# Attention for eight batches with a two-layer feed-forward: four heads in 32-row tiles, turned by 32x32 block transposes, laid out by a list scheduler

## The chip, the cores and the metric

One core of a Trainium2 chip runs the kernel. Its engines each work through an instruction queue of their own, in order: TensorE (PE in the profile; its weight loads are shown apart as PEld), VectorE (DVE), ScalarE (ACT), GpSimd (POOL), and SyncE (SP), which issues most DMAs. The metric is the device time of one execution in microseconds (us).

## What is computed

The reference, cut to what matters:

```python
# q, k, v: (8 batches, 12 heads, 448 tokens, 64); w_in: (768, 2048); w_out: (2048, 768)
q_n = q / np.sqrt(np.mean(q * q, -1, keepdims=True) + 1e-06) * g_q      # k_n likewise with g_k
scores = np.matmul(q_n, k_n.transpose(0, 1, 3, 2)) / 8
attn = softmax(scores)
x = np.matmul(attn, v).transpose(0, 2, 1, 3).reshape(3584, 768)
h = x @ w_in
out = (np.maximum(h, 0) + alpha * np.minimum(h, 0)) @ w_out
```

## The kernel before

**Groups.** The twelve heads of a batch are worked on in three groups of four (`G = 3`), so there are 24 groups, numbered y = 0 to 23; the tokens form seven blocks of 64 (`J = 7`). For a group, `load_qk` brings q and k to SBUF with one DMA each on SP's queue, `square` squares them (mostly POOL), `reduce` sums over the 64 elements of a head (VectorE), `root` makes 1/rms (ScalarE), and `scale` multiplies (POOL, for the first groups VectorE). The scaled `qs` must then be turned, with the head's 64 elements on partitions, into `qkT`. Group 0 has its own versions with the prefix `part_`.

**Turning.** For y below 7 (`TD`) TensorE transposes 14 blocks per group against the identity into a PSUM bank (lines 256, 285, 330), and VectorE copies the banks out, q with a copy (272, 291, 337) and k with a multiply by the combined gain (266, 295, 339). From y = 7 on `turn_dma` (line 304) issues two DMA transposes from SP, and `turn` multiplies k by the gain in place (line 315).

**Attention.** `score` (line 357) makes, for one group and one block of 64 keys, four heads' scores against all 448 queries: four matmuls of 64 rows by 64 columns of the array up to y = 8, and eight of 64 by 32 from y = 9 (`EARLY`). They run side by side. `soft` (371) is the exponential on ScalarE. `over_keys` (382) multiplies the exponentials by ones, which gives the denominators (`den`, tile `dn`), or by v (`attv`, tiles `av` and `avb`), in tiles of 64 rows by 32 columns. Two groups of a batch are summed as a pair, the third alone; for the third one `ones_over` (406) works on half the columns. `log` and `invert` (434, 439, 429) make 1/denominator on ScalarE, and VectorE multiplies it in and writes `xT` (464, 481).

**Feed-forward.** `up(b, ft)` (line 496) is six full-array matmuls for 128 of the 2048 hidden columns of batch b, in bank `hT` (or `hTa`, `hTb`); ScalarE multiplies by alpha (536) and VectorE takes the larger of the two (540) into `gT`, which holds two batches. `down` (558) is a direct product of 16 matmuls for a tile of 128 tokens and half of the output columns. From tile 6 on, pairs of tiles share seven half products of eight matmuls instead of eight (`quad_a`, `quad_b`, `quad_c`, and `quad` for the last tiles; line 623); POOL and VectorE make the sums that these need (`mix_two`, `mix_rest`, `mix_weights`). Results go out through tiles `osb` and SP.

**Order.** The work is written out burst by burst: each burst n holds two, seldom three or four, score tiles and perhaps a denominator or a value sum, and `gaps[n]` holds the feed-forward units behind it, given by a count of time for batches 0 and 1 and by a table after that. `prep`, `post`, `jobs`, `late` and `after` place the work of the other engines. Five direct products stand between batch 0's and batch 1's hT. Before the data is there TensorE runs `spin` matmuls on zeros.

PSUM has two tiles of two banks for scores (`sc`), one of two banks for sums (`acc`), and two of one bank (`mm`).

Of the kernel before, what the change touches and what calls it, by code (L numbers as in the profile page):

```python
# [21 lines left out]
def kernel(  # L22
# [18 lines left out]
    HH = H // 2  # L41
    G = HH // 2
# [6 lines left out]
    TD = min(7, NG)  # L49
    EB = 3  # L50
    EARLY = 3 * G
    PRE = 3 * G - 1
    assert G == 3

# [11 lines left out]
    q4, k4, v4 = (  # L66
        t.rearrange("b (h g) (p j) d -> b (g p) h (j d)", g=2, j=J) for t in (q, k, v)
    )
    out4 = out.rearrange("(b p j) m -> b j p m", b=B, j=J)

# [10 lines left out]
    cols = cst.tile([128, NF + 2], FP32, name="cols", tag="cols")  # L81
    alpha_sb = cols[:, :NF]
    gain = cst.tile([128, 1], FP32, name="gain", tag="gain")
# [11 lines left out]
    MIXED = 2 * G + 1  # L95
    arena = cst.tile([128, (3 * HB + 3 * SB) // 4], FP32, name="arena", tag="arena")

    def lent(start, size):

        return arena[:, start // 4 : (start + size) // 4]  # L100
# [5 lines left out]
    nat, sqs, qs, ss_t, rr_t, qkT, vt, xT = {}, {}, {}, {}, {}, {}, {}, {}  # L106
    SRC = {"q": q4, "k": k4}


    rows = lent(0, 512)[: NF + 2]  # L110

    def load_qk(y, hold=False):
        b, i = divmod(y, G)
        for nm in "qk":
            if y in (2, 5, 8):
                t = lent(HB + "qk".index(nm) * NB4, NB4).rearrange(
                    "p (h j d) -> p h j d", h=2, j=J
                )
            else:
                t = ld.tile([128, 2, J, D], FP32, name="nat", tag="nat", bufs=4)  # L120
            if hold and nm == "q":

                nc.scalar.copy(out=t[:, 0, 0, 0:1], in_=expb)
            o = t.rearrange("p h j d -> p h (j d)")
            for h in range(2) if (y, nm) == (0, "q") else (slice(0, 2),):
                nc.sync.dma_start(out=o[:, h], in_=SRC[nm][b, :, ds(2 * i, 2)][:, h])
            nat[y, nm] = t

    def load_v(b):
        t = att.tile([128, HH, J, D], FP16, name="vt", tag="vt", bufs=1)  # L130
        nc.gpsimd.dma_start(out=t.rearrange("p h j d -> p h (j d)"), in_=v4[b])
        vt[b] = t

    def block_of(g, i):
        return 2 * g + i if i < 2 else 4 + g

    def load_w_in(c):

        src = moe_w_in[:512].rearrange("(n x p) f -> n p x f", n=4, p=32)
        for n in range(4):  # L140
            nc.gpsimd.dma_start(
                out=w_in_sb[ds(32 * n, 32), :4, ts(c, FB)], in_=src[n, :, :, ts(c, FB)]
            )
        if c % 2 == 0:
            w = ts(c // 2, 2 * FB)
            src = moe_w_in[512:].rearrange("(n g e p) f -> e n p g f", n=2, g=2, e=2)
            for e in range(2):
                for n in range(2):
                    nc.gpsimd.dma_start(
                        out=w_in_sb[ds(64 * e + 32 * n, 32), 4:, w], in_=src[e, n, :, :, w]  # L150
                    )
# [11 lines left out]
    def square(y, nm):  # L163
        src = nat[y, nm].rearrange("p h j d -> p (h j d)")
        if y % 2 and y < 3 * G + 1:
            sq = lent(HB + (2 + "qk".index(nm)) * NB4, NB4).rearrange("p (n d) -> p n d", d=D)
        else:
            sq = ld.tile([128, 2 * J, D], FP32, name="sq", tag="sq", bufs=2)
        sqf = sq.rearrange("p n d -> p (n d)")
        if (y, nm) == (1, "q"):  # L170
            nc.scalar.activation(out=sqf, in_=src, func=AF.Square)
        else:

            n = 2 if (y, nm) in ((2, "q"), (G, "k")) else 1
            for h in range(n):
                c = ts(h, 2 * J * D // n)
                nc.gpsimd.tensor_mul(out=sqf[:, c], in0=src[:, c], in1=src[:, c])  # L177
        sqs[y, nm] = sq

    def reduce(y, nm, heads=None):  # L180
        if y not in ss_t:
            ss_t[y] = ld.tile([128, 2, 2, J], FP32, name="ss", tag="ss", bufs=4)
        o = ss_t[y][:, "qk".index(nm)].rearrange("p h j -> p (h j)").unsqueeze(2)
        for c in [slice(0, 2 * J)] if heads is None else [ts(h, J) for h in heads]:
            nc.vector.tensor_reduce(  # L185
                out=o[:, c], in_=sqs[y, nm][:, c], axis=AXIS_X, op=ALU.add
            )

    def root(y, nms="qk"):
        n = len(nms)  # L190
        at = "qk".index(nms[0])
        if at == 0:
            rr_t[y] = ld.tile([128, 2, 2, J], FP32, name="rr", tag="rr", bufs=4)
        rr, ss = rr_t[y][:, ds(at, n)], ss_t[y][:, ds(at, n)]
        nc.scalar.activation(out=rr, in_=ss, func=AF.Ln, scale=1.0 / D, bias=RMS_EPS)
        nc.scalar.activation(out=rr, in_=rr, func=AF.Exp, scale=-0.5)

    def scale(y, nm):
        if y in (1, 3, 5):
            t = lent(HB + 4 * NB4 + "qk".index(nm) * NB4 // 2, NB4 // 2).bitcast(FP16)  # L200
            t = t.rearrange("p (j h d) -> p j h d", j=J, h=2)
        else:
            t = ld.tile([128, J, 2, D], FP16, name="qs", tag="qs", bufs=2)
        eng = nc.vector if y < G or (y, nm) == (G, "q") else nc.gpsimd
        eng.tensor_mul(  # L205
            out=t.rearrange("p j h d -> p h j d"),
            in0=nat[y, nm],
            in1=rr_t[y][:, "qk".index(nm)].unsqueeze(3).broadcast_to((128, 2, J, D)),
        )
        qs[y, nm] = t  # L210


    tops = {}

    def part_square(nm, h, j, eng):
        if ("sq", nm) not in tops:
            tops["sq", nm] = ld.tile([128, 2 * J, D], FP32, name="sq", tag="sq", bufs=2)
        o = tops["sq", nm].rearrange("p (h j) d -> p h j d", h=2)[:, h, j]
        src = nat[0, nm][:, h, j]
        if eng is nc.scalar:  # L220
            nc.scalar.activation(out=o, in_=src, func=AF.Square)
        else:
            eng.tensor_mul(out=o, in0=src, in1=src)

    def part_reduce(nm, h, j):
        if 0 not in ss_t:
            ss_t[0] = ld.tile([128, 2, 2, J], FP32, name="ss", tag="ss", bufs=4)
        nc.vector.tensor_reduce(
            out=ss_t[0][:, "qk".index(nm), h, j].unsqueeze(3),
            in_=tops["sq", nm].rearrange("p (h j) d -> p h j d", h=2)[:, h, j],  # L230
            axis=AXIS_X, op=ALU.add,
        )

    def part_root(nm, j):
        if 0 not in rr_t:
            rr_t[0] = ld.tile([128, 2, 2, J], FP32, name="rr", tag="rr", bufs=4)
        n = "qk".index(nm)
        rr, ss = rr_t[0][:, n, :, j], ss_t[0][:, n, :, j]
        nc.scalar.activation(out=rr, in_=ss, func=AF.Ln, scale=1.0 / D, bias=RMS_EPS)
# [154 lines left out]
    def cols_of(ys):  # L394
        return S // 2 if halved(ys) else S
# [834 lines left out]
```

## Time and profile before

| | |
|---|---|
| median of 2 runs (range) | 413.1 us (412.56 to 413.63) |
| profiled execution: time, span | 414.78 us, 413.0 us |
| mean granted TensorE clock | 0.995 |
| instructions: TensorE, VectorE, ScalarE, GpSimd | 5055, 420, 390, 184 |
| one exponential (line 371), 168 of them | 913 ns |
| slope and max of one hT (lines 536, 540) | 633 and 623 ns |
| one square, one scale on POOL (177, 205) | 1681 and 1713 ns |
| one reduce on VectorE, 896 elements (185) | 1077 ns |
| copy of a turned q, gain multiply of a turned k from PSUM (337, 339) | 621 and 676 ns |
| gain multiply of k turned by DMA (315), 17 of them | 1135 ns |
| DMA transposes, 17 of q and 17 of k, to landing | 2.9 and 3.7 us |
| loads of q or k, 448 KB, to landing | 4.9 to 8.5 us |

The span runs from the first to the last instruction of the profiled execution. A row of instructions gives the mean duration of one. Since matmuls overlap, their durations add to more than the time that they take; the distance from one start to the next says more. A name in brackets behind a row is what ended the engine's idle time before it.

### The profile page before, as it was taken

How to read it: one execution, taken by the hardware profiler on the slowest of the kernel's cores; microseconds unless marked ns; L12 is line 12 of the kernel's file. 1: busy time of each engine (PE TensorE's matmuls, PEld its weight loads, DVE VectorE, ACT ScalarE, POOL GpSimd, SP SyncE). 2: the span in 40 equal slices, each digit the busy share in tenths (PEclk: the TensorE clock that was granted, in tenths of full speed). 3: DMA queues.
4: the chain of work that ended last, by engine and by line, in shares of the span. 5: the costliest groups of instructions: out<-in, count | busy, mean ns of one | idle time of the engine just before them, and what ended most of it. 6: DMA issues, size and time to landing. Idle time of an engine off the chain costs nothing.

```text
span 413.0 us, 11724 instructions
## 1 busy us (share of the span) xinstructions
PE 398.9 (97%) x5055; PEld 208.1 (50%) x5055; DVE 266.9 (65%) x420; ACT 257.3 (62%) x390; POOL 255.8 (62%) x184
## 2 busy tenths in 40 slices
PE   7889999899999999999999999999999999999996
PEld 3344445444456445554455445545555455645664
DVE  3876875476567388785688585958576755465322
ACT  5697787567846785557766786875657783135110
POOL 5599996589677969376373847484724407300870
PEclk9899999999999999999999999999999999999999
DMA  8999899957754894329861697279332700320143
GB/s 259 231 217 206 172 200 155 248 169 103 163 81 134 204 169 91 115 63 197 144 168 48 173 138 177 63 180 193 59 75 54 127 3 24 75 59 0 30 103 97
DMA packets 67330, 53.38 MB, mean 129 GB/s; under 512 B 34880, under 2 KB 66768, under 8 KB 67280
## 3 DMA queue, kind: packets, MB, share of 16 engines
q1 hardware_dynamic: 53344, 40.45, 40.5%
q0 software_dynamic: 13536, 11.81, 21.5%
q8 instruction: 39, 0.64, 0.7%
q10 hardware_dynamic: 400, 0.39, 0.3%
q14 instruction: 11, 0.09, 0.1%
HBM read 45.62 MB, written 11.01 MB: 137 GB/s over the span
## 4 chain that ended last, share of the span: by engine, by line
PE 49%; DVE 6%; ACT 0%; issue 0%; DVEq 0%
PE hT L496 14%; PE hTa L496 7%; PE qx L623 5%; PE sc L357 3%; PE oq L623 3%; PE qc L623 3%; PE qz L623 2%; PE av L382 2%; PE oqm L623 2%; PE avb L382 1%; PE dn L382 1%; PE oqa L623 1%; DVE ss L185 1%; DVE xT L481 1%; DVE kT L315 1%; PE qza L623 1%
## 5 line engine op out<-in xcount | busy, mean ns | idle before, releaser
L371 ACT ACTIVATE expT<-sc 128x896 f16<-128x896 f32 x168 | 147.8, 913 | 55.4 <-PE sc L357 55.0
L496 PE MATMUL hT<-xT,w_in_sb 128*128 128x448 f16 x546 | 113.7, 353 | 0.4 <-DVE gT L540 0.2
L496 PEld LDWEIGHTS <-w_in_sb 128*128 128x128 f16 x768 | 72.7, 98 | 74.8 <-issue 10.1
L540 DVE TENSOR_TENSOR gT<-hT,gT 128x448 f16<-128x448 f32 x91 | 56.6, 623 | 40.1 <-ACT gT L536 39.2
L205 POOL TENSOR_TENSOR qs<-nat,rr 128x896 f16<-128x896 f32 x36 | 60.9, 1713 | 33.4 <-issue 24.9
L536 ACT ACTIVATE gT<-hT,cols 128x448 f16<-128x448 f32 x90 | 56.9, 633 | 33.9 <-PE hT L496 33.7
L177 POOL TENSOR_TENSOR sq<-nat 128x896 f32<-128x896 f32 x32 | 53.1, 1681 | 38.0 <-DMA nat<-in_q_dram 25.3
L357 PE MATMUL sc<-qT,kT 64*32 64x448 f16 (+1 forms) x1092 | 53.3, 358 | 3.5 <-ACT expT L371 1.1
L623 PEld LDWEIGHTS <-gT 128*128 128x128 f16 x352 | 33.4, 98 | 26.0 <-issue 4.9
L496 PE MATMUL hTa<-xT,w_in_sb 128*128 128x448 f16 x210 | 45.4, 352 | 0.0
L185 DVE TENSOR_REDUCE ss<-sq 128x14 f32<-128x896 f32 (+1 forms) x37 | 38.3, 1052 | 0.6 <-POOL sq L177 0.6
L481 DVE TENSOR_TENSOR xT<-av,rden 64x448 f16<-64x448 f32 (+1 forms) x37 | 27.2, 734 | 13.5 <-PE av L382 5.5
L536 ACT ACTIVATE gT<-hTa,cols 128x448 f16<-128x448 f32 x35 | 22.2, 635 | 19.1 <-PE hTa L496 19.1
L540 DVE TENSOR_TENSOR gT<-hTa,gT 128x448 f16<-128x448 f32 x35 | 21.8, 624 | 17.7 <-ACT gT L536 17.6
L357 PEld LDWEIGHTS <-kT 64*32 64x32 f16 (+1 forms) x1092 | 15.6, 93 | 34.7 <-issue 29.3
L558 PE MATMUL op<-w_out_sb,gT 128*128 128x384 f16 x160 | 27.4, 326 | 0.0
L382 PEld LDWEIGHTS <-vt 64*32 64x32 f16 x1344 | 20.2, 92 | 14.1 <-issue 5.0
L611 POOL TENSOR_TENSOR gs<-gT 128x1024 f16<-128x1024 f16 x3 | 6.4, 2121 | 30.3 <-DVE gT L540 28.1
L558 PEld LDWEIGHTS <-gT 128*128 128x128 f16 x192 | 18.0, 98 | 13.5 <-issue 2.4
L382 PE MATMUL av<-expT,vt 64*32 64x448 f16 x896 | 24.3, 350 | 0.3 <-DVE osb L671 0.3
L619 POOL TENSOR_TENSOR gT<-gT 128x1024 f16<-128x1024 f16 x11 | 23.8, 2166 | 0.0
L623 PE MATMUL qx<-w_out_sb,gT 128*128 128x384 f16 x120 | 20.9, 326 | 0.0
(148 smaller groups left out, 494.1 us busy)
## 6 DMA issues: line engine op xcount, KB each, us to landing
out_dram<-osb SPq DMA_DIRECT2D x107, 96.0 KB, 2.8
nat<-in_k_dram SPq DMA_DIRECT2D x21, 448.0 KB, 5.4
nat<-in_q_dram SPq DMA_DIRECT2D x20, 448.0 KB, 4.9
vt<-in_v_dram POOLq DMA_DIRECT2D x8, 672.0 KB, 11.0
w_in_sb<-in_moe_w_in_dram POOLq DMA_DIRECT2D x24, 128.0 KB, 5.0
w_out_sb<-in_moe_w_out_dram POOLq DMA_DIRECT2D x4, 768.0 KB, 10.8
arena<-in_q_dram SPq DMA_DIRECT2D x3, 448.0 KB, 7.8
arena<-in_k_dram SPq DMA_DIRECT2D x3, 448.0 KB, 8.5
```

What stands on the lines that cost most here:

```text
L177: nc.gpsimd.tensor_mul(out=sqf[:, c], in0=src[:, c], in1=src[:, c])
L185: nc.vector.tensor_reduce(out=o[:, c], in_=sqs[y, nm][:, c], axis=AXIS_X, op=ALU.add)
L205: eng.tensor_mul(out=t.rearrange("p j h d -> p h j d"), in0=nat[y, nm], in1=rr_t[y][:, "qk".index(nm)].unsqueeze(3).broadcast_to((128, 2, ...
L357: nc.tensor.matmul(out=sc[ds(64 * g + m * c, m), par, :S].rearrange("p (j c) -> p j c", j=J), lhsT=kT[ds(64 * par, 64), j, g, ts(c, m)], r ...
L371: nc.scalar.activation(out=expT[y][:, j], in_=scs[y, j][:, :, :S], func=AF.Exp, scale=QK_SCALE, bias=EXP_BIAS,)
L382: nc.tensor.matmul(out=accs[g][ds(32 * n, 32), :S], lhsT=weights(g, y, par, c, j), rhs=expT[y][ds(64 * g, 64), j, par, :], start=(j == 0), ...
L481: nc.vector.tensor_mul(out=x, in0=av, in1=r)
L496: nc.tensor.matmul(out=hT[:, :S], lhsT=w_in_sb[:, block_of(g, i), ts(ft, 128)], rhs=xT[b][:, g, i, :], start=(i == 0 and g == 0), stop=(i ...
L536: nc.scalar.activation(out=g, in_=hT[:, :S], func=AF.Copy, scale=alpha_sb[:, ft : ft + 1])
L540: nc.vector.tensor_max(out=g, in0=hT[:, :S], in1=g)
L558: nc.tensor.matmul(out=op[:, :OH], lhsT=gT[:, ft, ts(tile % J, 128)], rhs=w_out_sb[:, ft, ts(oh, OH)], start=(ft == 0), stop=(ft == NF - 1),)
L623: nc.tensor.matmul(out=bank[:, c], lhsT=g[:, ft], rhs=v[:, ft, c], start=(first and ft == 0), stop=(ft == HF - 1), skip_group_check=True,)
```

## The change

Nearly the whole kernel is written anew around three parts.

**Layout.** q and k come in with 32 partitions per head, each with 14 tokens in a row (3.5 KB). `scale` writes tokens in pairs, so that two f16 values fill a 32-bit word, and `flip` turns 32x32 blocks of such words with one VectorE transpose per tensor and group. The head's 64 elements then lie in two halves (e = 0, 1) on the 32 partitions of that head. `weigh_k` multiplies k by the gain, one VectorE instruction per half (`WEIGHS` names VectorE for all). No TensorE or DMA transposes of q and k are left.

**Attention.** A score tile T covers two key blocks (s and s + 3) of four heads: 16 matmuls of 32 rows by 64 columns, in which the two halves e accumulate; it fills both `sc` tiles, and two exponentials follow. The seventh key block of two neighbouring groups makes a tile H. The sums take 128 rows by 32 columns for the T tiles (part 0) and 64 rows by 32 for the H tile (part 1). Groups are summed in pairs across batches, (0,1), (4,5) to (22,23), and 2 and 3 alone. v is loaded in two DMAs of 64 partitions per batch, with the middle block twice.

**Order.** Each piece of work is an `op` with an engine, a duration, its predecessors and a rank. `arrange` plays all engines forward in time and emits the instructions in the order that this gives. On TensorE it takes the next attention burst when enough feed-forward time (`RATE`, `RATE_1`) has passed since the last, and else the next of `units`, whose order is fixed. It counts 0.12 us where the tile shape changes. In `pair_tiles` each tile is a burst of its own; the sums of a pair ride behind the first three tiles of the next pair, or, for `OWN_END` and the last pair, stand alone. Opening tiles are issued in two halves. `hold` and `keep` are small VectorE copies that make the loads of y = 1, 2 and of 5, 6 wait. q of group 0 is loaded from SP in two halves, k of group 0 from ScalarE's queue. Slopes are all on ScalarE, and two hT of batch 0 are begun before its third group is done, where four were.

The planner's durations are 0.38 for a T tile, 0.875 for an exponential, 0.58 for a slope, 0.55 for a max, 0.5 to 0.52 for a result, 1.0 for a reduce, 0.58 for a flip, 0.6 for both gain multiplies.

```diff
-    q4, k4, v4 = (
-        t.rearrange("b (h g) (p j) d -> b (g p) h (j d)", g=2, j=J) for t in (q, k, v)
-    )
...
+    flat = {
+        nm: t.rearrange("b (i h) (p t) d -> b i (h p) (t d)", h=4, p=32)
+        for nm, t in (("q", q), ("k", k))
+    }
+    v4 = v.rearrange("b h (p j) d -> b p h (j d)", j=J)
...
-            nc.tensor.transpose(
-                tp[:, j, :], qs[y, nm][:, j].rearrange("p h d -> p (h d)"), ident
-            )
...
-    def turn_dma(y):
-        for nm in "qk":
-            t = att.tile([128, J, 2, 64], FP16, name=f"{nm}T", tag=f"{nm}T", bufs=3)
-            nc.sync.dma_start(
-                out=t.rearrange("p j g c -> p j (g c)"),
-                in_=qs[y, nm].rearrange("p j h d -> p (j h d)"),
-                transpose=True,
-            )
-            qkT[y, nm] = t
...
-        if y >= TD:
-            t = qkT[y, "k"].rearrange("p j g c -> p (j g c)")
-            nc.vector.tensor_scalar(
-                out=t, in0=t, scalar1=gain[:, 0:1], scalar2=None, op0=ALU.mult,
-                op1=ALU.max, accum_out=mark32,
-            )
-            return
...
-    def score(y, j):
-        qT, kT = qkT[y, "q"], qkT[y, "k"]
-        sc = pss.tile([128, 2, 512], FP32, name="sc", tag="sc")
-        m = 64 if y < EARLY else 32
-        for c in range(64 // m):
-            for par in range(2):
-                for g in range(2):
-                    nc.tensor.matmul(
-                        out=sc[ds(64 * g + m * c, m), par, :S].rearrange(
-                            "p (j c) -> p j c", j=J
-                        ),
-                        lhsT=kT[ds(64 * par, 64), j, g, ts(c, m)],
-                        rhs=qT[ds(64 * par, 64), :, g, :],
-                        start=True,
-                        stop=True,
-                    )
-        scs[y, j] = sc
...
-    def over_keys(accs, ys, weights):
-
-        heads = [(y, par, c) for y in ys for c in range(3 - len(ys)) for par in range(2)]
-        for j in range(J):
-            for n, (y, par, c) in enumerate(heads):
-                for g in range(2):
-                    nc.tensor.matmul(
-                        out=accs[g][ds(32 * n, 32), :S],
-                        lhsT=weights(g, y, par, c, j),
-                        rhs=expT[y][ds(64 * g, 64), j, par, :],
-                        start=(j == 0),
-                        stop=(j == J - 1),
-                    )
...
+        eng.tensor_mul(
+            out=qs[y, nm].rearrange("p (j d h) -> p h j d", j=J, h=2)[:, :, js],
+            in0=nat[y, nm][:, :, js],
+            in1=r.unsqueeze(3).broadcast_to((128, 2, count, D)),
+        )
...
+    def flip(y, nm, js=slice(0, J)):
+        if (y, nm) not in qkT:
+            qkT[y, nm] = att.tile([128, 2, J, 64], FP16, name=f"{nm}T", tag=f"{nm}T", bufs=3)
+        t = qkT[y, nm].rearrange("p e j c -> p (e j c)").bitcast(FP32)
+        nc.vector.transpose(
+            out=t.rearrange("p (e j c) -> p j e c", e=2, j=J)[:, js],
+            in_=qs[y, nm].bitcast(FP32).rearrange("p (j e c) -> p j e c", e=2, j=J)[:, js],
+        )
...
+                eng.tensor_scalar(
+                    out=t[:, e], in0=t[:, e], scalar1=gain[:, e : e + 1], scalar2=None,
+                    op0=ALU.mult,
+                )
...
+    def score(key, halves):
+        kind, y, s = key
+        for n in halves:
+            scs[key, n] = pss.tile([128, 2, 512], FP32, name="sc", tag="sc")
+        for e in range(2):
+            for n in halves:
+                for g in range(2):
+                    p = ds(32 * (2 * n + g), 32)
+                    sc = scs[key, n][:, g, :S]
+                    if kind == "T":
+                        todo = [
+                            (sc[ds(64 * m, 64)], qkT[y, "k"][p, e, s + 3 * m, :], y)
+                            for m in range(2)
+                        ]
+                    else:
+                        todo = [
+                            (sc[ds(64 * (z % 2), 64)], qkT[z, "k"][p, e, last_block(z)[0], :], z)
+                            for z in s
+                        ]
+                    for o, w, z in todo:
+                        nc.tensor.matmul(
+                            out=o, lhsT=w, rhs=qkT[z, "q"][p, e].rearrange("p j c -> p (j c)"),
+                            start=e == 0, stop=e == 1,
+                        )
+
...
+    def over_keys(acc, ys, weights, part):
+        for t in range(3) if part == 0 else ():
+            for y in ys:
+                s = slots_of(y)[t]
+                for a in range(4):
+                    nc.tensor.matmul(
+                        out=acc[y][ds(32 * a, 32), :S], lhsT=weights(slice(0, 128), y, a, s),
+                        rhs=ex["T", y, s][:, a], start=t == 0, stop=False,
+                    )
+        for a in range(4) if part else ():
+            for y in ys:
+                p = ds(64 * (y % 2), 64)
+                nc.tensor.matmul(
+                    out=acc[y][ds(32 * a, 32), :S], lhsT=weights(p, y, a, last_block(y)[1]),
+                    rhs=ex["H", y // 2][p, a], start=False, stop=True,
+                )
...
+    OWN_END = (4,)
+    TAIL_AT = (0, 1, 2)
+    MIDDLE = (("H", 1, (2, 3)),)
+    LATER = ()
+    BEGUN = {(0, 0), (0, 1)}
+    SLOPES = set()
+    KEPT = {5: ("x", 0, 0), 6: ("mx", 0, 4)}
+    W_RANK = (15.5, 22.5, 22.7, 23.5, 23.7, 24.5, 25.0, 25.5)
+    RATE, RATE_1 = 2.4, 1.4
+    SPINS = 15
+    SPIN_TO = 40.0
...
+    SETS = [(0, 1), (2,), (3,)] + [(y, y + 1) for y in range(4, NG, 2)]
...
+            if a.name[1] in opening or a.name[0] == "fill":
+                return (a, "att") if sa <= su + 0.05 else (u, "unit")
+            if state["since"] + 0.45 * u.dur >= goal and sa <= su + 0.3:
+                return a, "att"
+            if su <= sa or state["since"] < goal:
+                return u, "unit"
+            return a, "att"
...
+            switch = 0.0 if state["mode"] == o.mode else 0.12
...
+    def hold():
+        for nm in "qk":
+            nat[1, nm] = ld.tile([128, 2 * J * D], FP32, name="nat", tag="nat", bufs=4)
+        nc.vector.tensor_copy(
+            out=nat[1, "q"][:, 0:1], in_=nat[0, "q"].rearrange("p h j d -> p (h j d)")[:, 0:1]
+        )
...
+    def pair_tail(st):
+        d, a = den_ops(st), av_ops(st)
+        return [d, a[:2], a[2:]]
+
+    waiting = []
+    for y in range(4, NG, 2):
+        for n, key in enumerate(pair_tiles[y]):
+            burst = tile_ops(key, False)
+            if waiting and n >= waiting[0][0]:
+                burst = burst + waiting.pop(0)[1]
+            bursts.append(burst)
+            if y == 4 and n == 2:
+                bursts += late[(3,)]
+        parts = pair_tail((y, y + 1))
+        if y in OWN_END or y == NG - 2:
+            bursts += parts
+        else:
+            waiting = list(zip(TAIL_AT, parts))
...
+    units = side + [("ub", 0), ("ub", 1)] + U(0, 0, NF) + U(1, 0, NF)
+    units += [("d", t, oh) for oh in range(2) for t in range(6 - oh)]
+    units += [("d", 5, 1)] + U(2, 0, NF)
+    table = (
+        "a6 b6 c6 a8 b8 u16 c8 a10 b10 c10 u14 a12 b12 u2 c12 u9 a14 u3 b14 u4 a16 c14 b16 c16 "
+        "u16 a18 b18 c18 a20 b20 c20 u16"
     )
...
+    def weights(macro):
+        w = sum(n[0] == "S" for n in macro)
+        if macro[0][0] == "S" and macro[0][1] in opening:
+            return 0.0
+        return (RATE if macro[0][0] != 'S' or macro[0][1][1] > 9 else RATE_1) * w
+
+    load_order = arrange(attention + bursts, units, opening, weights, None)
```

## The prediction

> **What bounds the kernel now.** I read the page's engine shares and its 40 slices first, then the chain of waits in order of time, the timeline of the opening, the groups by shape, and last the waits of TensorE's weight loads.
>
> ```profile
> PE 398.9 (97%) x5055; PEld 208.1 (50%) x5055; DVE 266.9 (65%) x420; ACT 257.3 (62%) x390; POOL 255.8 (62%) x184
> PE   7889999899999999999999999999999999999996
> ```
>
> TensorE is busy nearly throughout and nothing else passes 65%. Since the ends of matmuls are modelled, I count its work by start-to-start distances, which the chain gives:
>
> ```profile
> 205.07 0.50 PE sc L357 x16
> 205.58 1.32 PE dn L382 x56
> 206.90 0.19 PE sc L357 x8
> 207.09 2.71 PE qc L623 x16
> ...
> 236.54 0.50 PE sc L357 x16
> 237.04 1.24 PE hT L496 x6
> 238.29 1.13 PE hTa L496 x6
> ```
>
> Eight score matmuls run side by side in 0.19 us: call that a pass. Two passes should take 0.38 but take 0.50, and the first hT behind them takes 1.24 where the next takes 1.13: each change between full-array products and small-tile attention costs 0.11 to 0.12 us. Between sc and dn, which have the same tile shape (64x32) here, nothing is lost: 0.19.
>
> ```profile
> PEld L357 <- issue: 29.3, 81, 0.9
> PEld L496 <- issue: 10.1, 29, 0.5
> PEld L623 <- issue: 8.6, 23, 0.7
> PEld L558 <- issue: 2.4, 9, 0.4
> ```
>
> The middle number counts such changes: 81 into scores, 29+23+9 = 61 back into full-array work. Adding changes inside attention (64x64 to 64x32), the timeline of TensorE has 135 from 33.95 us, where the first hT starts.
>
> TensorE's whole work by rows: 128 hT of 1.135 = 145.3; 12 direct products of 2.60 = 31.2; 77 half products of 1.30 = 100.1; 392 passes of 0.189 (168 scores, 56 dn, 168 av/avb) = 74.1; 8 narrow denominators of 0.80 = 6.4; 98 transposes, 0.79 per 14, = 5.5. Sum 362.6 of a span of 413.0. Of the missing 50.4, 22.9 lie before 33.95 (11.1 of work is done there), 3.9 behind the last matmul at 409.1, and 23.6 between: 135 changes at 0.115 = 15.5, and 8.1 of real waits.
>
> ```profile
> 7.41 1.04 ACT L221 ACTIVATE sq<-nat 128x384 f32<-128x384 f32 x2 [1.67 <-DMA nat<-in_k_dram]
> 11.58 0.57 PE L357 MATMUL sc<-qT,kT 64*64 64x448 f16 x8 [0.87 <-DVE kT L266]
> 33.95 1.69 PE L496 MATMUL hT<-xT,w_in_sb 128*128 128x448 f16 x8
> 39.40 1.09 DVE L481 TENSOR_TENSOR xT<-av,rden 128x896 f16<-128x896 f32 x1 [2.94 <-ACT rden L439]
> ```
>
> The opening is a chain: k lands, is normalized and turned, the first score starts at 11.58, ScalarE's exponentials pace the rest, and xT of batch 0 is whole at 40.49.
>
> The profiled execution took 414.8 us (span 413.0 and 1.8 around it), 1.7 above the median 413.1. I sum on 414.8 and take 1.7 off at the end.
>
> **The change part by part.**
> *TensorE's work.* Scores stay 168 passes (84 tiles of two), hT, products and exponentials (168) keep their counts. Eleven pairs of 21 passes and two single groups of 12 replace eight pairs of 21 and eight singles (7 passes and 0.80): 48.2 against 49.1, -0.9. The transposes leave; of the 5.5, the three turns after 33.95 (47.4, 58.9 and 62.8) are 2.4 on the path, the others stand in the opening's idle time: -2.4. No row shows 32-row tiles; both shown small shapes give 0.19 a pass for 8 and for 4 tiles, and I keep it (a pass of 0.25 would cost 168 x 0.06 = 10; no row with 448 columns is under 0.19). The eleven opening tiles come in halves of two passes each, 11 x 0.38 = 4.2 more, in the opening's idle time.
>
> *Changes of shape.* The old order gives scores and sums one shape from y=9, and puts 2 to 4 passes in a burst. The new one has scores in 32x64, sums in 128x32 and their last block in 64x32. From the first hT: 73 tiles, each its own burst, 146 changes; eight pairs whose three tails ride on tiles, two more changes each, 48; the single y=3 6, and pairs 4 and 22 alone, 9 each. Together 218 against 135: 83 x 0.115 = +9.5. Changes among small shapes have a row: 64x64 scores at 35.57 give way to dn at 35.88, 0.31 for a pass of 0.19. A change between 32 and 128 rows has none; its bounds are 0 and twice the row, so 56 x 0 or 56 x 0.23, -6.4 or +6.4 on the sum; I take the row.
> [...]
>
> *VectorE.* It loses: copies of transposes, 7 x 0.62 and 5.1 for k; the gain multiply L315, 17 x (1.135+0.08) = 20.7; L425, 4.1; and of xT's 36.5, 7.0, since 44 rows of 0.62 and two of 1.09 remain. It gains 48 block transposes: 448 32-bit words per partition each, nearest L481 with 128x448 f32 at 0.62 (bounds 0.39, the 224-word copy L425, and 1.08, the 896-element reduce L185), 28.8 at 0.60; and 48 gain multiplies of 448 f16: bounds 0.31 (half of L337) and 0.57 (half of L315), 19.2 at the 0.40 of L266 with 384. 267 becomes 274, at worst 305 (74%): no bound. What hides it is TensorE's queue of products; in the opening nothing does.
>
> *DMA.* 34 DMA transposes of 2.9 and 3.7 to landing leave SP's queue, which also issues loads and stores; runs of q and k double to 3.5 KB; v grows by a seventh. In the list of waits TensorE waits for a DMA only at the gains' transpose (1.3, in the opening) and at 33.95 (0.2): 0. POOL loses L279 and the issue of the gains (to SP) and keeps its squares and scales.
>
> *The opening.* k is issued by ScalarE behind its table load (ends 2.02). The loads of y=1 and 2 wait for a VectorE copy that follows q's landing, those of y=5 and 6 for first values of batch 0's xT and gT; behind them on SP stand only further loads, the first store coming after 64, and behind the copy on VectorE only reduces that need q. q took 2.7 from issue to use, so k lands between 4.7 and the old 7.4; 5.5 taken. Squares 1.15, last reduce 0.65, root 0.45, scale q 1.09, flip 0.60, k's first piece 0.95, gaps 0.2: first score about 10.6, 1.0 earlier. From there ScalarE has 22 exponentials (20.1), roots 1.35, logs and inverses 3.0, a square 0.9: 36.0 if never idle, xT at 37.4; it did idle before, so 39 against 40.5. But two hT instead of four are begun before, 8 x 0.189 = 1.5 less done: 0, with -3 and +3 as ends.
>
> *Between batch 0 and 1.* The old order puts five direct products (at 63.6, 68.6, 76.7, 81.2, 86.2) before batch 1's hT at 89.4. The new list puts all of them behind batch 1's hT, so from 39 to batch 1 ScalarE leads: 20 exponentials 18.3, 16 slopes 10.1, logs and inverses 3.0, roots 1.4, end of chain 1.2: 73. TensorE has 16.7 of hT, 6.2 of tiles with their changes, 6.9 of sums: 4.2 idle, where the old order waited 2.8: +1.4.
>
> *Waits later.* 5.3 remain in the old order. The new one is computed with 0.55 for the max (row 0.62), 0.875 for the exponential (0.91), 0.52 for results (0.56): what TensorE waits for comes 4 to 13% later than planned. Bounds: 0 and three times 5.3; I take half as much again, +2.7.
>
> Sum: 414.8 - 0.9 - 2.4 + 9.5 + 0 + 1.4 + 2.7 = 425.1; less 1.7: **423 us**.
>
> **The rivals.**
> *A, the order closes the waits (faster).* Place: TensorE's 8.1 of waits and ScalarE's idle time in the opening. If a list made from all durations removes the 8.1 and the opening ends at 37.4 (-3), and the 56 changes inside a burst cost nothing, then 414.8 - 3.3 - 8.1 - 3 + 3.1 = 403.5, 402 on the median. For it: the chain shows late VectorE work (L664 to L671 behind qz, 220.2 to 222.7) that an earlier place would spare. Against: TensorE's own gaps are 8.1 in all. It needs all three; above 405 it isn't decided.
> *B, shapes cost, waits vanish (no change).* 414.8 - 3.3 + 9.5 - 8.1 + 0 = 412.9, 411. For it: later products depend on attention done long before.
> *C, VectorE late (much slower).* Flips at 1.08 and gains at 0.57 add 31 us to an in-order engine that ends every product; in the opening and up to batch 1 (eight groups of 1.3, 10.4) this is bare, and the rest hides: 434. For it: windows 20 to 60 show VectorE already 64 to 84% busy. Against: the nearest row is 0.62.
> [...]
>
> **How the numbers follow.** Forecast 0.45 (its own range 415 to 431), A 0.15, B 0.2, C 0.2. The range, 403 to 435, takes in B, the edge of A and C's mean. Two per cent, about what a measurement of this kernel can tell from no change, is below 404.8 and above 421.4. Faster: A, 0.15. Within: B and the forecast's lower part, 0.28. Slower: the rest of it and C, 0.57.
>
> **What would show it.** First score near 10.6 and xT of batch 0 whole near 39; about 218 changes of tile shape at 0.11 to 0.12, also from 32x64 to 128x32; flips near 0.6; a stretch near 65 to 73 where hT waits for batch 1's xT. Wrong, if changes inside bursts cost nothing, if a score tile takes more than 0.4, or if TensorE waits for VectorE in the products.

## The result and the profile after

The changed kernel takes 479.2 us (median of 2 runs, 478.9 to 479.5) against 413.1: a ratio of 1.160, 95% interval 1.153 to 1.167. The forecast was 423, the range ended at 435. The profiled execution has a span of 477.6.

The page of the kernel after, parts 1 and 2, as they were shown of before:

```profile
PE 428.9 (90%) x4126; PEld 199.1 (42%) x4126; DVE 309.5 (65%) x457; ACT 257.4 (54%) x382; POOL 265.1 (55%) x179
...
PE   6586799688889898789999988899899999999996
...
PEclk9658599699989898999999998999999999999999
```

TensorE is still the busiest engine but has lost 7 points, and there are holes in its first ten slices, where the granted clock falls to 0.5. VectorE's share stays at 65% (309.5 us busy, where 274 was forecast and 305 at worst): by its share alone it is no bound, as the prediction said. The groups by shape say otherwise. The columns are busy time, mean ns of one, idle time before:

```profile
L213 DVE TENSOR_SCALAR kT<-kT,gain 128x448 f16<-128x448 f16 x44 | 51.9, 1218 | 0.3
L199 DVE STREAM_TRANSPOSE qT<-qs 128x448 f32<-128x448 f32 x21 | 13.3, 635 | 5.7 <-POOL qs L189 4.0 <-PE sc L272 1.5
```

The flip is what was forecast (0.635 for 0.60). The gain multiply was priced at 0.40 and takes 1.22 on average. What makes it so long stands in the timeline (start, duration, both multiplies of one group in a row), with GpSimd's rows of the same stretches:

```profile
31.95 0.78 DVE L213 TENSOR_SCALAR kT<-kT,gain 128x448 f16<-128x448 f16 x2
...
123.95 4.12 DVE L213 TENSOR_SCALAR kT<-kT,gain 128x448 f16<-128x448 f16 x2
...
354.97 0.58 DVE L213 TENSOR_SCALAR kT<-kT,gain 128x448 f16<-128x448 f16 x2
```

```profile
31.19 1.46 POOL L229 DMA_DIRECT2D w_in_sb<-in_moe_w_in_dram  x2
...
122.72 3.33 POOL L164 TENSOR_TENSOR arena<-nat 128x896 f32<-128x896 f32 x2
126.00 1.68 POOL L164 TENSOR_TENSOR sq<-nat 128x896 f32<-128x896 f32 x1
```

At 31.95 GpSimd only issues transfers and at 354.97 it does nothing: two multiplies take 0.6 to 0.8. At 123.95 they start beside a row of three squares and end 0.4 behind the last of them (127.68): taken singly, the first takes 3.88, up to 127.83, and the second 0.32. Sorted by whether arithmetic of GpSimd overlaps them, the 44 multiplies take 0.35 (11 free) and 1.51 (33 beside it, the longest 5.12). The maxes (one operand in PSUM) take 0.62 free and 0.61 beside it, the reduces of 896 elements 1.075 either way, the flips of 448 words 0.63 and 0.62.

This falls on the path. The chain of waits (start, duration) and the list of waits (total, times, longest) of the kernel after:

```profile
288.00 0.62 DVE gT L399
288.62 0.55 DVE qT L199
289.17 0.53 DVE kT L199
289.70 0.62 DVE gT L399
290.32 4.06 DVE kT L213 x2
294.38 0.54 DVE gT L399
294.92 0.04 issue
294.96 2.29 PE hT L373 x6
```

```profile
PEld L272 <- DVE kT L213: 16.0, 9, 4.1
...
PE sc L272 <- DVE kT L213: 11.9, 7, 3.8
...
PE hT L373 <- DVE gT L399: 4.0, 6, 2.0
```

The max behind the multiplies (294.38) is what frees the bank for the next hT. Scores wait for the multiplies directly, and products through the maxes queued behind them.

The opening, in windows of the kernel after (width, busy time and count of PE, PEld, DVE, ACT, POOL; then clock, DMA share, GB/s):

```profile
10.00:20.00 10.00, 3.52 (x40) 1.11 (x40) 9.08 (x17) 3.37 (x4) 7.43 (x6) 0.76 0.32 112
20.00:30.00 10.00, 7.57 (x61) 1.85 (x54) 8.58 (x17) 6.53 (x11) 7.98 (x10) 0.50 0.76 153
30.00:40.00 10.00, 8.89 (x104) 2.27 (x95) 3.98 (x6) 6.71 (x9) 8.49 (x9) 0.54 1.23 186
```

xT of batch 0 is whole at 61.2 (40.5 before), and TensorE runs at about half clock from 20 to 40 (0.50 and 0.54). From 84.15 to 100.91 it has only scores and sums before batch 1's first hT.

To place the loss I use one sum: the time at which a given amount of TensorE's work is done, less that work (448 columns of the whole array counted as 0.187, where both traces have 0.189 from start to start, a small tile its share of that, spins left out). All work is 356.9 before and 351.0 after.

| time not spent on work | up to 30 us of work | from 30 to 50 | from 50 to 350 |
|---|---|---|---|
| before | 26.4 | 4.0 | 21.5 |
| after | 51.9 | 14.6 | 56.1 |
| after, gains on ScalarE | 47.7 | 10.3 | 36.7 |
| the same, loads, products and v moved (last experiment) | 44.1 | 9.4 | 33.2 |

Opening +25.5, the stretch around batch 1 +10.6, all the rest +34.6, less 5.9 of work: 64.8, the difference of the spans (64.6).

### The profile page after: what moved, and what is told of

Same layout as the page of the kernel before. It is cut to its first block, busy times and chain, and to the rows that moved or that the text cites. A ratio compares the mean times of both kernels' runs of the same rounds, so it can differ in the third digit from the quotient of the medians.

```text
span 477.6 us, 9828 instructions
## 1 busy us (share of the span) xinstructions
PE 428.9 (90%) x4126; PEld 199.1 (42%) x4126; DVE 309.5 (65%) x457; ACT 257.4 (54%) x382; POOL 265.1 (55%) x179
## 3 DMA queue, kind: packets, MB, share of 16 engines
q0 software_dynamic: 20000, 12.59, 18.8%
## 5 line engine op out<-in xcount | busy, mean ns | idle before, releaser
L272 PE MATMUL sc<-qT,kT 32*64 32x448 f16 x1344 | 66.3, 396 | 26.3 <-ACT expT L283 12.0
L189 POOL TENSOR_TENSOR qs<-nat,rr 128x896 f16<-128x896 f32 (+2 forms) x39 | 63.1, 1641 | 47.0 <-DVE qT L199 23.8
L399 DVE TENSOR_TENSOR gT<-hT,gT 128x448 f16<-128x448 f32 x91 | 55.9, 618 | 40.1 <-ACT gT L388 39.8
L164 POOL TENSOR_TENSOR sq<-nat 128x896 f32<-128x896 f32 x32 | 53.9, 1688 | 24.3 <-DMA nat<-in_q_dram 14.9
L213 DVE TENSOR_SCALAR kT<-kT,gain 128x448 f16<-128x448 f16 (+3 forms) x58 | 57.7, 1037 | 0.4
L373 PE MATMUL hTa<-xT,w_in_sb 128*128 128x448 f16 x222 | 49.5, 358 | 3.2 <-DVE gT L399 3.2
L170 DVE TENSOR_REDUCE ss<-sq 128x14 f32<-128x896 f32 (+1 forms) x40 | 40.7, 1029 | 13.6 <-POOL sq L164 12.4
L272 PEld LDWEIGHTS <-kT 32*64 32x64 f16 x1344 | 17.4, 107 | 67.6 <-issue 46.5
L388 ACT ACTIVATE gT<-hTa,cols 128x448 f16<-128x448 f32 x37 | 23.5, 634 | 22.5 <-PE hTa L373 22.4
L399 DVE TENSOR_TENSOR gT<-hTa,gT 128x448 f16<-128x448 f32 x37 | 22.8, 617 | 18.8 <-ACT gT L388 18.7
L446 POOL TENSOR_TENSOR gs<-gT 128x1024 f16<-128x1024 f16 x3 | 6.3, 2122 | 47.8 <-DVE gT L399 47.8
L341 DVE TENSOR_TENSOR xT<-av,rden 128x448 f16<-128x448 f32 x22 | 12.7, 617 | 16.9 <-PE av L300 16.9
L293 PEld LDWEIGHTS <-vt 128*32 128x32 f16 x576 | 14.3, 99 | 22.2 <-issue 15.8
L178 ACT ACTIVATE rr<-ss 128x28 f32<-128x28 f32 x24 | 5.4, 225 | 32.8 <-DVE ss L170 32.8
## 6 DMA issues: line engine op xcount, KB each, us to landing
w_in_sb<-in_moe_w_in_dram POOLq DMA_DIRECT2D x12, 256.0 KB, 10.6
```

The source lines that it names most:

```text
L170: nc.vector.tensor_reduce(out=ss_t[y][:, n_of(nm), c].unsqueeze(2), in_=sqs[y, nm].rearrange("p (n d) -> p n d", d=D)[:, c], axis=AXIS_X, ...
L189: eng.tensor_mul(out=qs[y, nm].rearrange("p (j d h) -> p h j d", j=J, h=2)[:, :, js], in0=nat[y, nm][:, :, js], in1=r.unsqueeze(3).broadca ...
L213: eng.tensor_scalar(out=t[:, e], in0=t[:, e], scalar1=gain[:, e : e + 1], scalar2=None, op0=ALU.mult,)
L272: nc.tensor.matmul(out=o, lhsT=w, rhs=qkT[z, "q"][p, e].rearrange("p j c -> p (j c)"), start=e == 0, stop=e == 1,)
L373: nc.tensor.matmul(out=hs[b, ft][:, :S], lhsT=w_in_sb[:, 2 * i + e, ts(ft, 128)], rhs=xT[b][:, i, e], start=start and n == 0 and e == 0, s ...
L388: nc.scalar.activation(out=g_of(b, ft), in_=hs[b, ft][:, :S], func=AF.Copy, scale=alpha_sb[:, ft : ft + 1],)
```

## The experiments

Every kernel was run beside the kernel before on the same chip (412.5 to 413.4); each number is a median, with the ratio's interval.

**The gain multiplies.** Four kernels. On the kernel after, the multiply in the form that also accumulates:

```diff
-    scalar2=None, op0=ALU.mult,
+    scalar2=None, op0=ALU.mult, op1=ALU.max, accum_out=mark32,
```

> The gain multiplies of k on VectorE take the accumulating form that the kernel before used (a second operation and an accumulator output); order and durations in the planner unchanged. Theory 1 (the plain multiply waits while GpSimd works: 348 ns free, 1508 ns beside it): each multiply takes about 0.6 us whether GpSimd works or not, VectorE loses some 25 us of busy time, and the time falls to 435 to 455. Theory 2 (the loss is the order, the opening and TensorE's half clock, and VectorE's time is hidden): the multiplies change as said but the time stays above 468.

Then with no multiply at all (`weigh_k` returns at once, the gains are left out of k, the order stays):

> The gain multiplies of k are left out (k is not weighted, so the output is that of attention without gains); the planner still lays out the order with them. Theory 1: the time falls at least as far as in e1, to 430 to 450. Theory 2: above 468.

Then the kernel before, with its own multiply of k in the plain form:

```diff
-                op1=ALU.max, accum_out=mark32,
```

> The kernel before, with its 17 gain multiplies of k behind the DMA transposes in the plain form, without second operation and accumulator. Theory 1: they go from 1135 ns each to about 0.5 us where GpSimd is idle and 1 to 3 us beside it, mean above 1.2 us, and the time rises by 2 to 12 us. Theory 2: the plain form is only shorter, mean 0.3 to 0.6 us, and the time stays within 1 us or falls.

Then the kernel after with the multiplies on ScalarE, the order laid anew:

```diff
-    WEIGHS = {(y, n): "DVE" for y in range(NG) for n in range(4)}
+    WEIGHS = {}
```

> The changed kernel with the gain multiplies on ScalarE (two activations per group, planned at 1.1 us) and the order planned anew. Theory 1: ScalarE gains some 27 us of work (to 60% busy) and the time still falls, to 435 to 460. Theory 2: the time stays above 468.

Measured: 455.9 (1.100 to 1.109), 451.5 (1.085 to 1.102), 419.5 (1.008 to 1.025) and 451.1 (1.089 to 1.097). The first two end 0.9 and 1.5 above theory 1's ranges and far under theory 2's 468; the other two lie in theory 1's. The groups by shape, first of the accumulating kernel, then of the kernel before with the plain form (the accumulating form had 1135 there):

```profile
L214 DVE TENSOR_SCALAR_CACHE_REDUCE kT<-kT,gain 128x448 f16<-128x448 f16 x44 | 29.7, 675 | 1.1
```

```profile
L315 DVE TENSOR_SCALAR kT<-kT,gain 128x896 f16<-128x896 f16 x17 | 24.0, 1414 | 0.0
```

The same arithmetic in another form of instruction is 23.2 faster, though it is twice as long as a free plain multiply (0.675 against 0.35). The plain form makes the kernel before 6.8 slower. Without any multiply 27.6 are gained, so at least 23.2 of the 66 is the waiting for GpSimd (the other form is itself the longer one where nothing is waited for), and about 4 the multiplies themselves. Some 38 remain open, and the kernel with the gains on ScalarE (451.1) is the base for the rest.

**The tile shapes.** One matmul of 32 columns ahead of each of 126 hT, in a 32x64 tile or, as a control, in a 128x128 one:

```diff
+    nc.tensor.matmul(out=hs[b, ft][:64, :32], lhsT=ident[:32, :64],
+                     rhs=ident[:32, :32], start=True, stop=True)
     up_part(b, ft, range(G), True, True)
```

> Base: the same 451.1 kernel. A matmul of 32 columns in a 32x64 tile is put ahead of each of 126 hT products; at 89 of them it stands between two full-size products (two more changes of the tile shape each) and at 17 behind a 64x32 tile (one more): 195 more changes. Theory 'shape': a change costs 0.11 to 0.13, so this is 21 to 25 slower than the run beside it, whose added matmuls are full-size. Theory 'none': no cost but the matmul's own, and both take the same.

> As the run beside it, but the added matmul of 32 columns is 128x128, the shape of the product behind it: no more changes between products; 0.02 to 0.05 each, so 453 to 458 by either theory.

Measured: 475.2 (1.148 to 1.152) and 456.2 (1.102 to 1.106). The timelines of TensorE have 409 and 213 changes from 40 us on: 196 more cost 19.0, 0.097 each, a little under the 21 to 25 of theory 'shape'. Changes among the small shapes cost as well. In the chain of the kernel after six passes of 128x32 sums take 1.25 and one pass of 64x32 sums 0.31, against 6 x 0.189 = 1.13 and 0.19 without a change (the passes of before):

```profile
395.86 1.25 PE av L293 x24
397.11 0.31 PE av L300 x8
397.42 1.25 PE avb L293 x24
```

The prediction counted 218 changes from the first hT on, against 135. Counted in the same way, the kernel after has 204 (from 59.95 on); from 87 to 93, for instance, tile follows tile with no product between. So 69 more, not 83, and at 0.097 to 0.115 the term is 6.7 to 7.9 for the 9.5 forecast.

**The opening and the stretch behind it, one edit at a time on the base.** Weight transfers behind group 3's squares:

```diff
-    W_RANK = (15.5, 22.5, 22.7, 23.5, 23.7, 24.5, 25.0, 25.5)
+    W_RANK = (15.5, 23.5, 23.7, 24.5, 24.7, 25.5, 26.0, 26.5)
```

> Base: the changed kernel with the gain multiplies on ScalarE (451.1). Here only the ranks of the weight transfers change, so that on GpSimd's queue the squares of group 3 come before eight of the twelve issues of moe_w_in. Theory 'queue': the tile of both groups 2 and 3 must be done before the denominators of group 2, and its chain starts with group 3's squares, which in the base begin at 32.84 behind 27.52 to 32.82 of DMA issues (4.6 busy). So the squares begin at about 27.6, xT of batch 0 is whole at 52 to 53 instead of 57.3, and the time is 446 (445 to 448). Theory 'clock': the scores at half clock are what is late, so xT is whole within 1.5 of 57.3 and the time within 1.5 of 451.

Idle matmuls behind the opening's half tiles of scores:

```diff
+        if free and o.name[0] == "S":
+            spin(3, False, True)
```

> Base: the same 451.1 kernel. Here three idle 128x448 f16 matmuls follow each half tile of scores until the first denominators, to hold TensorE's clock; all else keeps its order. Theory 'clock': the granted clock of 20 to 40, 0.57 to 0.60 in the base, comes to 0.9 or more, 16 score matmuls start in 0.8 to 1.0 instead of 1.6 to 1.8 all told, xT of batch 0 is whole at 50 to 53 instead of 57.3, and the time is 444 to 447. Theory 'queue': the clock rises but group 3's squares still begin near 32.8, xT is whole within 1.5 of 57.3, and the time stays at 450 to 452. Should the added matmuls stand in the way at half clock (0.37 each, 36 to 60 of them), it is slower, by up to 6.

Direct products between batch 0 and 1:

```diff
-    units = side + [("ub", 0), ("ub", 1)] + U(0, 0, NF) + U(1, 0, NF)
+    units = side + [("ub", 0), ("ub", 1)] + U(0, 0, NF) + early + U(1, 0, NF)
```

> Base: the same 451.1 kernel. Here five of the direct products of batch 0 (tiles 0 to 2) stand between the hT of batch 0 and those of batch 1, as in the kernel before; they are taken from the stretch behind batch 1. Theory 'gap': the base loses 9.7 of 20 in 80 to 100, where TensorE has only scores and waits for batch 1's xT; with 13 of products there it loses 3 to 4 and the time is 444 to 447. Rival: the products are missing later, where the attention is again ahead of nothing, and the loss only moves: time within 1.5 of 451.

> All three edits on the same base of 451.1: weight transfers later, matmuls that hold the clock, five direct products between batch 0 and 1. If opening and gap are the rest of the loss, and add up, xT of batch 0 is whole at 45 to 48 and the time is 433 to 440. If the shapes and waits behind 100 are the larger part, 443 or more.

Measured: 456.8 (1.103 to 1.111), 453.1 (1.092 to 1.100), 454.3 (1.097 to 1.106) and 453.7 (1.096 to 1.103). None gained: the gains that 'queue', 'clock' and 'gap' each forecast did not come, and of the third pair the rival is the nearer. Yet the edits did what they were for. With the weights later the squares of group 3 began at 27.56, as meant, but xT of batch 0 came at 56.2 and not at 52 to 53, and the kernel became 5.7 slower, which neither theory had. The window from 20 to 30, of the base and then with the idle matmuls:

```profile
20.00:30.00 10.00, 8.01 (x64) 2.10 (x63) 6.49 (x10) 8.99 (x20) 9.40 (x11) 0.60 1.01 189
```

```profile
20.00:30.00 10.00, 9.98 (x82) 3.43 (x84) 6.10 (x9) 8.39 (x19) 8.10 (x10) 0.98 1.06 197
```

The clock was nearly full (0.98 for 0.60) and xT of batch 0 came at 56.6 instead of 57.3, with no gain in time. So idle matmuls in this opening brought the clock up, and that alone did not help; whether the idle matmuls took back a part of what the clock gave was not separated. The mark itself scatters: in the base, the kernel with five products between and the two kernels of the tile shapes, every engine has the same instructions in the same order up to there, and xT of batch 0 was whole at 57.3, 58.4, 55.9 and 54.7 in the one execution profiled of each. Differences below 3.7 in it say little, and the first column of the table above scatters as much among these four. With the products between, the stretch from 80 to 100 went from 14.9 to 18.8 busy, and the one from 150 to 180 from 28.3 to 23.8: the wait moved behind batch 1, where the products were then missing.

Two more kernels: one with the single edit of five idle matmuls instead of fifteen at the start (`SPINS`), and one with an order planned with the durations measured in the opening, which takes in several edits:

> Base: the changed kernel with the gain multiplies on ScalarE (451.1, span 449.8). Here five idle matmuls stand at the start of TensorE's queue instead of fifteen; nothing else moves. In the base the first two transposes of the gains wait behind them until 9.03, the copy of the gains on VectorE (9.35) waits for those, and the two reduces of group 0's k (9.42), whose squares are done at 6.8, stand behind the copy. Theory 'queue': the copy comes at about 6.5, the root of group 0 at about 7.9 instead of 10.59, the first exponential at 13.7 instead of 16.43, and as every later order is fixed, the end moves by the same 2 to 3: 448 to 449. Theory 'absorbed': the opening regains it at the next wait, and the time is within 1 of 451.1.

> Base: the same 451.1 kernel. Here the list scheduler is given the durations measured in the opening (pieces of k, transfers that GpSimd issues, gain multiplies), five instead of fifteen idle matmuls, idle matmuls behind the first half tiles of scores, six direct products of batch 0 between batches 0 and 1, and ranks, rates and squares chosen so that the scheduler's own end comes earlier: 402.2 against 409.3 with these durations and 404.5 in the base (before the last three tile pairs of products, about 31). Theory 'order': the base ran 15 over its scheduler's end with that tail (404.5 + 31), nearly all lost in the first 60, because the order was laid for durations that did not hold; with durations that hold, the kernel comes within 3 to 6 of 402 + 31: 436 to 439. Theory 'collisions': engines share something in the opening that no duration tells, and the time stays above 445.

Measured: 451.7 (1.091 to 1.094) and 453.7 (1.094 to 1.103). With fewer idle matmuls xT of batch 0 was whole at 53.9 (57.3 in the base, 55.9 and 54.7 in the two kernels of the tile shapes, which ran beside this one), and batch 2's at 168.7 after 169.5: what was won was gone by then. The replanned order, 2.3 shorter in the scheduler's own time, was no faster.

**What absorbs it.** Loads of q and k of groups 5 and 6 are held (`keep`) until batch 0 has got somewhere: a late opening makes the next groups late too.

```diff
-    KEPT = {5: ("x", 0, 0), 6: ("mx", 0, 4)}
+    KEPT = {}
```

> Base: the changed kernel with the gain multiplies on ScalarE and five idle matmuls at the start (451.7). Here the loads of q and k of groups 5 and 6 no longer wait for marks of batch 0 (the first piece of its xT, the fifth gT tile); the scheduler's own end does not move (404.6 against 404.5). Theory 'holds': a late opening delays these loads a second time, since in the base group 6 is issued at 64 and lands at 70 to 72, where the kernel before has it at 37 to 38, and GpSimd is idle from 60 to 74. So its loads land before 60, GpSimd is busy over 5 of 60 to 74, batch 2's xT is whole at 158 to 162 instead of 168.7, and the time is 441 to 446. Theory 'bandwidth': the weights land later by as much, batch 0 or the direct products wait for them, and the time is within 2 of 451.7.

> The run beside it with three direct products of batch 0 between the hT of batch 0 and 1 (scheduler's own end 400.5 against 404.6). Alone, five of them gained nothing (454.3 against 451.1), as the wait came back before batch 2. Theory 'holds': with batch 2 ready earlier the three fill the wait before batch 1 and none is missed later: 4 less than the run beside it, 437 to 442. Theory 'bandwidth': 451 or more.

> The second run with two more edits of the opening: v of batch 0 is issued on GpSimd's queue before group 0's pieces of k (the DMA engines' share is 0.32 in 10 to 20 of the base, 0.91 in the kernel before), and idle matmuls hold TensorE's clock (0.98 to 1.00 in 20 to 40 where that was done alone). Theory 'starved opening': the transfers behind v land 3 to 5 earlier, and the time is 433 to 438. Theory 'chain': the opening is bound by the chain through VectorE, ScalarE and GpSimd, not by data or clock: within 2 of the second run.

Measured: 454.5 (1.096 to 1.105), 448.5 (1.080 to 1.090), 444.0 (1.071 to 1.078). Freeing the loads alone costs 2.8, nearer to the rival: the loads came earlier (group 6 landed at 45.9 and 47.6 instead of 66.4 and 68.2), xT of batch 0 later (58.9 instead of 53.9), and batch 1 waited. Three direct products in that wait then gained 6.0, more than the 4 forecast, though 448.5 lies in neither theory's range; five products alone had gained nothing. Three products with the loads still held were not run, so it stays open whether the freed loads or the smaller number made the difference. The third kernel gained another 4.5, which is again between its two theories. It had two edits at once, so each was run alone:

> Base: the run without holds and with three direct products between (448.5). The run with two more edits of the opening took 443.97; this has one of them, the idle matmuls that hold TensorE's clock until the first denominators (base: 0.50 in 20 to 30, 0.67 in 30 to 40). Theory 'clock': 444 to 445, the whole gain. Theory 'data': 448 to 449, and the other run has the gain. When the rest of the opening was still as in the change, these matmuls alone gained nothing (453.1 against 451.1).

```diff
-    ... if b > 1 else [("sq", 2, "k", 0)], rank=...
+    ... if b > 1 else [("gm",)] if b == 0 else [("sq", 2, "k", 0)], rank=...
```

(`("gm",)` is the product of the two gains, early on GpSimd's queue; `("sq", 2, "k", 0)` the square of group 2's k.)

> The other of the two edits alone on the same base of 448.5: v of batch 0 issued on GpSimd's queue before group 0's pieces of k, with no added matmuls. Theory 'data': 444 to 445, with the DMA engines' share of 10 to 20 at 1.0 or more instead of 0.40. Theory 'clock': 448 to 449.

Measured: 450.0 (1.084 to 1.093) with the clock held, 444.1 (1.071 to 1.079) with v issued early. The whole gain is v's. The window from 10 to 20 of the run without, then with it:

```profile
10.00:20.00 10.00, 6.55 (x53) 1.74 (x54) 8.18 (x13) 6.83 (x17) 9.99 (x10) 0.70 0.40 138
```

```profile
10.00:20.00 10.00, 6.52 (x53) 1.71 (x53) 7.38 (x14) 6.81 (x17) 6.72 (x6) 0.72 1.11 208
```

The change puts v's and the weights' transfers behind the squares of group 2 on GpSimd. In the kernel before v is issued at 7.46, in the kernel after at 22.69; the rows of the two, and the window from 10 to 20 of the kernel before:

```profile
7.46 0.91 POOL L131 DMA_DIRECT2D vt<-in_v_dram  x1
22.69 1.57 POOL L221 DMA_DIRECT2D vt<-in_v_dram  x2
10.00:20.00 10.00, 8.62 (x67) 3.83 (x70) 8.18 (x14) 7.04 (x10) 5.38 (x7) 0.83 0.91 227
```

From 10 to 20 the DMA engines are at 0.91 of their time before and at 0.32 after. In the last kernel v is issued at 6.37 (17.96 in its base), and xT of batch 0 comes at 54.3 instead of 57.8, with the clock at 0.50 from 20 to 30 in both. One such pair could be scatter, but the five kernels without holds agree: 53.9 and 54.3 with v early, 57.8, 58.3 and 58.9 without. Whether v itself or the transfers behind it were missed was not separated.

No version came near the kernel before. The best stands 31 above it (28.7 in the spans): opening 17.7, the stretch around batch 1 5.4, and 11.7 behind it, of which the shapes are 7.0 to 8.3 (177 changes against 105 there); less 5.9 of work. What makes up the 17.7 was not separated further and stays open.

## Why the prediction was wrong

The way, slower, was forecast with 0.57, but for another reason than the one that decided: the shapes, the largest term, are some 7 of the 66 us, and VectorE and the opening, both put at 0, are most of the rest. That much is luck.

- *TensorE's work* (-3.3) and *changes of shape* (+9.5): right in sign, and near in size: -5.9 by the sum above, which counts the opening's transposes too, and 6.7 to 7.9. A change costs about what was taken for it (0.097 in the experiment), also among the small shapes (0.12 in the chain); there are 14 fewer.
- *VectorE* is the step that failed: "19.2 at the 0.40 of L266", with 0.57 as upper bound, "no bound" behind it, and TensorE's queue of products to hide it. The group has 57.7. The price of a free multiply was right (0.35); what was missing is the wait. The rows that it was taken from had an operand in PSUM (L266, 0.41 for 384 elements free and 0.48 for 512 beside GpSimd; L337, 0.62 in the free one and in the 4 beside it) or were of the accumulating form (L315, 1.135 in the 3 free ones and in the 14 beside GpSimd), and none of them shows such a wait. I took the element count for the likeness that matters. The traces show which forms wait: the plain multiply takes 0.35 free and 1.51 beside GpSimd, the accumulating one 0.675 on average over all 44, the reduces 1.075 either way; why one form waits and another does not was not shown. The wait can be longer than one instruction of GpSimd: the multiply at 123.95 stood for 3.88, until the third of a row was done, and the one of 5.12 us (195.05 to 200.17) through the rest of one and three more, the last of which ends at 200.03. Nor did TensorE's queue of products hide it: a max behind the multiplies holds a bank, and the next product waits (hT for maxes 4.0 in all, up to 2.0 at once).
- The trace of the kernel before had the sign. Its f16 mixes on VectorE read and write SBUF alone. They take 0.68 to 0.69 in the 11 free ones; of the 5 beside arithmetic of GpSimd one, which meets only the last 0.16 of a GpSimd multiply, takes 0.71, and the other four 1.59 to 2.06. Two of each, and GpSimd's row at the first two:

```profile
206.44 1.93 DVE L611 TENSOR_TENSOR arena<-gT 128x1024 f16<-128x1024 f16 x1
208.41 2.06 DVE L612 TENSOR_TENSOR arena<-arena,gT 128x1024 f16<-128x1024 f16 x1
243.32 0.68 DVE L611 TENSOR_TENSOR arena<-gT 128x1024 f16<-128x1024 f16 x1
244.04 0.69 DVE L612 TENSOR_TENSOR arena<-arena,gT 128x1024 f16<-128x1024 f16 x1
206.13 3.78 POOL L205 TENSOR_TENSOR qs<-nat,rr 128x896 f16<-128x896 f32 x2
```

- *DMA* (0) and *the opening* (0, -3 to +3): measured +25.5, the second failure. I looked for waits for DMAs in the list of before, where there were hardly any, and not at which transfer is now issued behind what. v's place alone is worth 4.4 once the loads and products are in place; the gains' share of the opening is 4.2, little above the scatter of 3.7. First score 12.63 for 10.6, xT whole at 61.2 for 39. Three scales of 896 elements on VectorE, priced at 1.09, took 1.57, 1.81 and 1.17, all beside GpSimd. The larger part of the 25.5 stays open.
- *Between batch 0 and 1* (+1.4): the stretch has +10.6, of which 4.3 goes where the gains are on ScalarE. The place was right, the start was not: batch 1's hT at 100.91 for 73, as the opening was late and held loads came later still. TensorE's clock fell there too (0.74 granted from 80 to 100).
- *Waits later* (+2.7): of the 34.6 behind 50 us of work, 7.0 to 8.3 are shapes, 19.4 go when the gains leave VectorE, and 7 to 8 remain, inside the bounds given (0 to 3 x 5.3, so up to 10.6 more) but over twice what was taken.
- *Rival C* named the right engine and the wrong instruction: the flips stayed at 0.63, and its 0.57 for the gains was less than half of the truth. A and B fell with the opening.

## What to carry to other kernels

Price a new VectorE instruction by a row of its own form, with its operands in the same memories and the same work on GpSimd beside it; an equal element count is not enough (448 elements took 0.35, 0.675 or 1.51 here). If no such row exists, sort the nearest group by whether GpSimd works beside it: a group with two durations for one shape is the warning. When TensorE idles in an opening, look at the share of the DMA engines and at what the transfers are queued behind before blaming the clock; here v's place gave 4.4 and the clock nothing. In an order fixed on all queues, a gain at one place can come back as a wait at the next (with five products between, TensorE was busy 3.9 longer from 80 to 100 and 4.5 shorter from 150 to 180), so a cause that shows no gain when mended alone is not yet refuted: here freed loads cost 2.8 alone, and with three products behind them the two together gained 3.2.

## What the hardware showed that was not expected

In the kernel after, a plain f16 multiply from SBUF to SBUF on VectorE took 0.35 us for 448 elements alone and 1.51 on average beside GpSimd arithmetic, up to 5.12. The mixes of f16 with two SBUF operands (1024 elements) show the same: 0.68 in the 5 free ones of L446, 2.0 in the 3 beside GpSimd. And holding TensorE's clock at or near full in the opening (from 20 to 30: 0.98 for 0.60, and 1.00 for 0.50) gained nothing in two kernels (453.1 for 451.1, 450.0 for 448.5).
